# Random-feature attention and two dense layers on one core: keys first, query chunks beside the first layer, and the first layer in two halves of its features

## The chip, the cores and the metric

The kernel runs on one core of a Trainium2 chip. The time is the device time of one execution in microseconds; three executions of the kernel before gave 988.63, 992.81 and 994.16, median 992.81. TensorE is called PE here, VectorE DVE, ScalarE ACT, GpSimd POOL and SyncE SP; all DMAs are issued by SP, in the order of its queue.

## The reference

Inputs are q, k, v (4 batches, 8 heads, 576 tokens, 64 wide), omega (128 by 64) and two pairs of weights. Attention is linear, with random features; then come two dense layers over 2304 tokens with 512 channels and 2048 hidden features, the first with h cos(h), the second with h relu6(h + 3) / 6.

```python
def phi(x):
    proj = np.einsum('bhsd,md->bhsm', x, omega)
    h = proj - np.sum(x * x, axis=-1, keepdims=True) / 2.0
    h = h - np.max(h, axis=-1, keepdims=True)
    return np.exp(h) / np.sqrt(m)
q_p, k_p = (phi(q_s), phi(k_s))
kv = np.einsum('bhsm,bhsd->bhmd', k_p, v)
z = np.sum(k_p, axis=2)
num = np.einsum('bhsm,bhmd->bhsd', q_p, kv)
den = np.einsum('bhsm,bhm->bhs', q_p, z)[..., None] + 1e-06
...
h = x @ w_in
g = h * np.cos(h)
...
g = h * np.clip(h + 3.0, 0.0, 6.0) / 6.0
return (g @ w_out).astype(np.float32)
```

The weights come as 64-bit floats and are turned into 32-bit ones bit by bit on the chip.

## The kernel before

**Precision.** The layers and the projection of the attention are made with operands split into a high part, rounded to the fp32r format, and a low part, the rest. One product is three matmuls: high with high, low weight with high, high with low.

**Attention.** The 2304 tokens are 18 chunks of 128. `att_unit` (L298) makes one unit: keys or queries of one chunk, four of the eight heads. It loads the chunk transposed (xT) and as it lies (nat), squares nat on ACT or POOL and sums it on DVE (sq), splits xT on POOL (th, tl), projects with six matmuls of 256 columns (L359, on an omega that stands twice, block by block on the diagonal), takes maxima (L369) and two bias steps (L373, L377) on DVE, and the exponentials on ACT (L388). A key unit ends in the sums kv over its tokens (L400), a query unit in transposes (L427), a copy (L430), numerators (L440), division (L450 to L461), and after both halves transposes (L475) into xx (L480), the input of the first layer. Queries run six chunks behind the keys, unit by unit interleaved.

**Layers.** A slot is one block of tokens with one chunk of 128 hidden features: 12 matmuls into h (L614), the function, 12 matmuls out of it (L697) that accumulate in four PSUM banks y over all 16 feature chunks of the block. Blocks of the first layer are 512, 512, 256, 512 and 512 tokens, of the second 512 four times and 256. The cosine costs nine steps (L630 to L684): two on ACT and one on DVE or ACT to find the number of turns, two on DVE to take it off, absolute value, sine and rounding on ACT, product and low part on DVE (low part on POOL in the first 16 slots). A weight half (512 columns) is a load of 512 KB, a magnitude (on ACT in the first layer), four steps on DVE (L532 to L548), the rounding wh on ACT and the low part wl on POOL (L569). The halves of 11 of the 16 feature chunks have their buffers where the attention's buffers were, so they are written after the last xx.

**Order.** Nothing is left to chance: `Plan` (L68) is a list scheduler that writes one order for all engines. Each task has a key, durations by engine, what it waits for, and ring buffers that it takes and frees; at each moment the free engine takes the ready task with the smallest key. BIAS shifts the keys of some kinds of tasks. On the chip each engine then runs its own list strictly in that order, waiting on semaphores.

## Time and profile before

| | us |
|---|---|
| median of three runs | 992.81 |
| the profiled execution, its span | 988.6 |
| PE, DVE, ACT, POOL busy | 946.7, 649.2, 497.1, 239.3 |
| first matmul of the first layer starts at | 145.2 |
| block 0 of the first layer, to the start of block 1 | 116.6 |
| each full block of the second layer from 672.1 on | 87.0 |

The span of the profiled execution is close to the fastest of the three runs. The slices show the span in 40 parts of 24.7 us. A window cut at the first matmul of each block shows how long the block took; PE's busy time says little, since the ends of pipelined matmuls are modelled, so matmuls are best read by the distance of their starts. The same holds for DVE and ACT, whose neighbouring instructions overlap in the timeline.

### The profile page before, as it was taken

The numbers are of one execution on the slowest core, as the hardware profiler recorded it, in microseconds if no ns is written. First come the engines' busy times: TensorE is split into PE (matmuls) and PEld (weight loads), VectorE is DVE, ScalarE is ACT, GpSimd is POOL, SyncE is SP. The second block draws the span as 40 slices with busy tenths as digits, with TensorE's granted clock in tenths as the row PEclk, the third lists the DMA queues.
The fourth block names the chain that finished last, engine by engine and source line by source line (L and its number), as shares of the span: only waits on it lengthen the run. The fifth ranks groups of instructions, "written<-read, shape, count | busy, mean of one in ns | idle before, by whom it ended". The sixth has DMA issues, their size and how long they took to land.

```text
span 988.6 us, 15131 instructions
## 1 busy us (share of the span) xinstructions
PE 946.7 (96%) x5714; PEld 792.7 (80%) x5714; DVE 649.2 (66%) x1267; ACT 497.1 (50%) x1010; POOL 239.3 (24%) x270
## 2 busy tenths in 40 slices
PE   8999799988799999999999999999999999999998
PEld 7888687766588889988887778788888888888898
DVE  7999998999995566755699999823223222322322
ACT  6888789666655455544455553323223322322332
POOL 7778844556510000000134234300000000000000
PEclk9999999999999999999999999999999999999999
DMA  9774422344330000000023324101000100100010
GB/s 342 245 237 150 129 63 88 107 128 130 104 107 0 1 1 2 1 1 1 1 59 94 104 73 141 43 0 43 1 1 1 43 1 0 43 1 1 1 43 23
DMA packets 25480, 63.11 MB, mean 64 GB/s; under 512 B 2752, under 2 KB 3776, under 8 KB 25408
## 3 DMA queue, kind: packets, MB, share of 16 engines
q1 hardware_dynamic: 25408, 62.15, 19.5%
q8 instruction: 45, 0.74, 0.3%
q14 instruction: 27, 0.22, 0.1%
HBM read 57.42 MB, written 4.72 MB: 63 GB/s over the span
## 4 chain that ended last, share of the span: by engine, by line
PE 60%; DVE 32%; issue 5%; ACT 2%; DMA 1%; SPq 0%; POOL 0%; DVEq 0%; ACTq 0%
PE h L614 28%; PE pt L697 14%; PE kv L697 14%; DVE wt L542 4%; DVE r L647 3%; DVE wt L532 3%; DVE mx L369 3%; DVE wt L548 3%; DVE wt L536 3%; DVE r L643 2%; DVE mx L373 2%; PE h L359 1%; DVE sq L334 1%; DVE wk L658 1%; DVE gl L257 1%
## 5 line engine op out<-in xcount | busy, mean ns | idle before, releaser
L614 PE MATMUL h<-mxl,wh 128*128 128x512 f32 (+1 forms) x640 | 237.0, 370 | 3.9 <-DVE mxl L257 3.9
L614 PE MATMUL h<-mxh,wl 128*128 128x512 f32 (+1 forms) x640 | 236.9, 370 | 2.1 <-POOL wl L257 2.0
L614 PE MATMUL h<-mxh,wh 128*128 128x512 f32 (+1 forms) x640 | 238.1, 372 | 0.2 <-ACT wh L250 0.2
L257 DVE TENSOR_TENSOR gl<-wk,gh 128x512 fp32r<-128x512 f32 (+1 forms) x144 | 93.8, 651 | 100.3 <-ACT gh L250 93.3
L250 ACT ACTIVATE gh<-wk 128x512 fp32r<-128x512 f32 (+1 forms) x160 | 93.8, 586 | 126.4 <-PE pt L697 101.9
L614 PEld LDWEIGHTS h<-mxl,wh 128*128 128x128 f32 x640 | 121.2, 189 | 26.1 <-DVE mxl L257 6.0
L675 DVE SCALAR_TENSOR_TENSOR wk<-wk,h 128x512 f32<-128x512 f32 (+1 forms) x80 | 50.8, 635 | 138.1 <-ACT wk L669 138.0
L614 PEld LDWEIGHTS h<-mxh,wl 128*128 128x128 f32 x640 | 121.5, 190 | 23.1 <-POOL wl L257 3.2
L614 PEld LDWEIGHTS h<-mxh,wh 128*128 128x128 f32 x640 | 121.5, 190 | 20.8 <-ACT wh L250 0.7
L252 POOL TENSOR_SCALAR mxh<-xx 128x512 fp32r<-128x512 f32 (+1 forms) x20 | 15.9, 799 | 494.2 <-PE h L614 273.3
L257 POOL TENSOR_TENSOR wl<-wt,wh 128x512 fp32r<-128x512 f32 x64 | 97.6, 1528 | 151.7 <-ACT wh L250 140.2
L697 PE MATMUL kv<-gl,wh 128*128 128x512 f32 (+1 forms) x320 | 119.5, 374 | 7.3 <-POOL gl L257 3.8
L697 PE MATMUL kv<-gh,wh 128*128 128x512 f32 (+1 forms) x320 | 118.9, 372 | 4.1 <-ACT gh L250 3.3
L697 PE MATMUL kv<-gh,wl 128*128 128x512 f32 (+1 forms) x320 | 118.7, 371 | 3.5 <-POOL wl L257 3.3
L669 ACT ACTIVATE wk<-h,three 128x512 f32<-128x512 f32 (+1 forms) x80 | 51.5, 644 | 138.7 <-PE h L614 138.7
L697 PE MATMUL pt<-gl,wh 128*128 128x512 f32 (+1 forms) x320 | 119.2, 373 | 0.0
L697 PE MATMUL pt<-gh,wl 128*128 128x512 f32 (+1 forms) x320 | 119.1, 372 | 0.0
L697 PE MATMUL pt<-gh,wh 128*128 128x512 f32 (+1 forms) x320 | 119.0, 372 | 0.0
L651 ACT ACTIVATE r<-r 128x512 f32<-128x512 f32 (+1 forms) x80 | 47.1, 589 | 112.8 <-DVE r L647 112.8
L388 ACT ACTIVATE P<-h,mx 128x128 f32<-128x128 f32 x288 | 81.4, 390 | 19.0 <-DVE mx L377 16.6
L658 DVE TENSOR_TENSOR wk<-h,r 128x512 f32<-128x512 f32 (+1 forms) x80 | 50.7, 634 | 46.2 <-ACT r L655 45.8
L697 PEld LDWEIGHTS kv<-gl,wh 128*128 128x128 f32 x320 | 60.3, 188 | 21.5 <-DVE gl L257 6.5
(70 smaller groups left out, 1583.2 us busy)
## 6 DMA issues: line engine op xcount, KB each, us to landing
ws<-w SPq DMA_DIRECT2D x64, 512.0 KB, 3.7
v<-vn SPq DMA_DIRECT2D x18, 260.0 KB, 4.7
nat<-kn SPq DMA_DIRECT2D x18, 256.0 KB, 4.0
nat<-qn SPq DMA_DIRECT2D x18, 256.0 KB, 3.7
xT<-qT SPq DMA_DIRECT2D x18, 256.0 KB, 3.2
xT<-kT SPq DMA_DIRECT2D x17, 256.0 KB, 4.7
yT<-xx SPq DMA_DIRECT2D x9, 256.0 KB, 2.6
yT<-xx SPq DMA_DIRECT2D x4, 512.0 KB, 2.7
```

What stands on the lines that cost most here:

```text
L250: nc.scalar.activation(out=o, in_=i, func=ACTF.Copy)
L257: (nc.gpsimd if e == "p" else nc.vector).tensor_tensor(out=o, in0=a, in1=b, op=ALU.subtract)
L369: nc.vector.tensor_reduce(out=mx[:, 0:4], in_=pj, axis=AX.X, op=ALU.max)
L388: nc.scalar.activation(out=p[:, o], in_=pj[:, o], func=ACTF.Exp, scale=SCALE, bias=mx[:, 8 + h:9 + h])
L532: nc.vector.tensor_scalar(out=w, in0=w, scalar1=F64_TINY, scalar2=F64_HUGE, op0=ALU.max, op1=ALU.min)
L542: nc.vector.scalar_tensor_tensor(out=u, in0=buf[("ws",) + W][:, :, 1], scalar=SIGN_HI, in1=u, op0=ALU.bitwise_and, op1=ALU.bitwise_or)
L614: nc.tensor.matmul(out=hb(), lhsT=w[:, 128 * kc:128 * kc + 128], rhs=x, start=(kc == 0 and j == 0), stop=(kc == KC - 1 and j == 2),)
L651: nc.scalar.activation(out=r, in_=r, func=ACTF.Abs)
L658: nc.vector.tensor_tensor(out=buf[WK][:, :n], in0=hb(), in1=buf[R_][:, :n], op=ALU.mult)
L669: nc.scalar.activation(out=tile_of(sb, WK, "wk", [128, 512])[:, :n], in_=hb(), func=ACTF.Relu, bias=three)
L675: nc.vector.scalar_tensor_tensor(out=w, in0=w, scalar=6.0, in1=hb(), op0=ALU.min, op1=ALU.mult)
L697: nc.tensor.matmul(out=buf["y", bi, ec][:, :n], lhsT=w[:, o], rhs=x, start=(f == 0 and j == 0), stop=(f == NF - 1 and j == 2),)
```

## The change

- **Stages.** All 18 key chunks run first, then the 18 query chunks, a whole chunk (8 heads) at a time. Beside the query chunks runs part of the first layer: the first 1024 tokens in four blocks of 256, for feature chunks 0 to 7, two feature chunks per "pair slot" in one PSUM bank (48 matmuls of 256 columns). A period is two query chunks; the sines of two pair slots follow the exponentials of their period and come before those of the next (`period`, `prior`, `sn_after`), so ACT changes its table twice a period.
- **Two halves.** The first layer is made for features 0 to 7 over all tokens (mode "pair" for the first 1024, "part" for 512, 512 and 256 more), and its half sums, scaled, go through yp to yy in DRAM; then features 8 to 15 (mode "add") load them back and add. Only the weights of features 8 to 15 (16 halves instead of 22) wait for the attention's buffers.
- **Attention.** No nat loads and no split: the squared sums come from PE (matmuls of the squared xT with a mask), the projection is eight plain fp32 matmuls of 128 columns on 64 rows each, the even heads from partitions 0 to 63 into one bank, the odd ones from 64 to 127 into another. Bias steps are once per chunk, 8 wide.
- **Cosine.** The attention's output is divided by 2 pi, h is in turns, and the cosine is two steps on DVE, a sine on ACT, product, rounding and low part; the factor comes back at the evacuation of y.
- **Weights.** The magnitude is always made on ACT, and wl may go to POOL or DVE; in the emitted order all of it is on DVE. POOL has 275 instructions before and 65 now.
- **Constants.** Rings and banks are divided anew, BIAS is empty, the table of units is gone.

```diff
+N_LATE = 8
+NG = NF - N_LATE
...
+T_K = 3.1
+T_Q = 17.0
...
+    "at": 2, "pt": 2, "h": 2, "kv0": 1, "kv1": 1, "ws": 3, "wt": 3, "mxh": 4, "mxl": 4, "wk": 3, "gh": 2, "gl": 2, "yp": 3,
 }
-Y_BANKS = ["kv0", "kv1"] + ["pt"] * (6 - N_H)
...
+Y_BANKS = ["kv0", "kv1", "h", "h"]
+BIAS = {}
...
+        def sums(e):
+            p = bank(S0, sr)
+            for i in range(4):
+                nc.tensor.matmul(
+                    out=p[:, i:8:4], lhsT=buf[SX][:, 128 * i:128 * i + 128], rhs=mask, start=True, stop=True,
+                )
...
+            for i in range(4):
+                for o in range(2):
                     nc.tensor.matmul(
-                        out=p[:, 256 * i:256 * i + 256], lhsT=w[:, 128 * i:128 * i + 128], rhs=x,
-                        start=(j == 0), stop=(j == 2),
+                        out=buf["pj", kind, c, o][:, 128 * i:128 * i + 128],
+                        lhsT=buf[X][64 * o:64 * o + 64, 128 * i:128 * i + 128],
+                        rhs=omd[64 * o:64 * o + 64, :], start=True, stop=True,
                     )
...
+    for c in range(NCH):
+        p = c // 2
+        prior = [("sn", g) for g in range(n_a) if period(g) == c // PER - 1]
+        chunk("q", c, t_q + T_Q * p + 3 * (c % 2), prior, 10)
...
+    blocks = [dict(m=1, t0=256 * b, n=256, fs=range(0, NG), mode="pair") for b in range(N_A)]
+    blocks += [dict(m=1, t0=t0, n=n, fs=range(0, NG), mode="part") for t0, n in ((1024, 512), (1536, 512), (2048, 256))]
+    n_g1 = len(blocks)
+    blocks += [dict(m=1, t0=t0, n=n, fs=range(NG, NF), mode="add") for t0, n in ((0, 512), (512, 512), (1024, 512), (1536, 512), (2048, 256))]
...
+        add(("wl",) + W, k, {"p": 1.5, "v": 0.68},
...
+            def r1(e):
+                w = buf[WK][:, :n]
...
+                nc.vector.scalar_tensor_tensor(out=w, in0=w, scalar=MAGIC, in1=hb(), op0=ALU.subtract, op1=ALU.subtract)
...
+        sn_after = [("e", "q", c, hf) for c in range(NCH) for hf in range(2) if c // PER == period(g)]
+        nonlinear(g, 1, k, 512, [("in", g, KC - 1)], sn_after + ([("sn", g - 1)] if g else []))
...
+                    nc.vector.scalar_tensor_tensor(
+                        out=xx[:, ec, t0:t0 + n], in0=buf["y", bi, ec][:, :n], scalar=TWOPI, in1=buf["yp", bi, ec][:, :n],
+                        op0=ALU.mult, op1=ALU.add,
+                    )
```

What the change does to the order is seen best on PE and ACT. PE before, where the first layer begins: the last projections of the attention (L359), transposes of finished queries (L475), the first slot (L614) and transposes of exponentials (L427).

```order
L359 MATMUL h<-omh,th 128x256
L359 MATMUL h<-oml,th 128x256
L359 MATMUL h<-omh,tl 128x256
L475 MATMUL pt<-ident,xn 128x128 x4
L614 MATMUL h<-mxh,wh_74 128x512
L614 MATMUL h<-mxh,wl_75 128x512
L614 MATMUL h<-mxl,wh_74 128x512
L427 MATMUL pt<-ident,P 128x128 x4
```

PE now, in the middle of the query stage, between two slots: L709 is a pair slot's matmul into h (wh_83 of slot 13, wh_85 of slot 14), L479 the transposes of query chunk 14, L325 the squared sums and L348 the projection of chunk 16, L431 the transposes and L444 the numerators of chunk 15.

```order
L709 MATMUL h<-mxl,wh_83 128x256
L479 MATMUL pt<-ident,xn 128x128 x4
L325 MATMUL pt<-mask,sqx 128x2 x4
L348 MATMUL at<-omd,xT 128x128 x8
L431 MATMUL pt<-ident,P 128x128 x8
L444 MATMUL pt<-kvs,qt 64x65 x16
L709 MATMUL h<-mxh,wh_85 128x256
L709 MATMUL h<-mxh,wl_86 128x256
L709 MATMUL h<-mxl,wh_85 128x256
```

After these come the other 15 of the 18 matmuls into h, 24 out of slot 12, transposes, 24 out of slot 13 and six more into h of slot 14. The attention's steps moved between the slots of the layer, where before all projections were over when the layer began.

ACT before, around the only change of its table after the start: the turns of the first slots (L637), roundings of weights (L250), copies (L480, L430), an absolute value (L651), the sine (L655).

```order
L637 ACTIVATE wk<-wk,nmagic 128x512
L250 ACTIVATE wh_74<-wt 128x512
L250 ACTIVATE wh_82<-wt 128x512
L480 ACTIVATE xx<-pt 128x4x128
L430 ACTIVATE qt<-pt 128x512
L651 ACTIVATE r<-r 128x512
L430 ACTIVATE qt<-pt 128x512
L655 ACT_TABLE_LOAD
L655 ACTIVATE r<-r,halfpi 128x512
```

ACT now, one period: exponentials (L386) of query chunks 14 and 15, squares (L318), copies of transposes and of finished queries (L249 qt, xx), the sines (L659) and roundings (L249 gh) of slots 12 and 13.

```order
L386 ACT_TABLE_LOAD
L386 ACTIVATE P<-at,mx 128x128 x8
L318 ACTIVATE sqx<-xT 128x512
L249 ACTIVATE qt<-pt 128x512 x2
L386 ACTIVATE P<-at,mx 128x128 x8
L249 ACTIVATE xx<-pt 128x4x128
L659 ACT_TABLE_LOAD
L659 ACTIVATE wk<-wk,halfpi 128x512
L249 ACTIVATE qt<-pt 128x512
L659 ACTIVATE wk<-wk,halfpi 128x512
L249 ACTIVATE gh<-wk 128x512 x2
```

The sines stand between the exponentials of two periods now, where before all exponentials were over. On DVE the two steps of slot 13 (L649, L655) stand ahead of the copy of the squared sums of chunk 16 (L330), its maxima (L361) and a copy of transposes (L253).

```order
L465 TENSOR_TENSOR xn<-pt,rd 128x4x64
L458 RECIPROCAL rd<-rd 128x4
L465 TENSOR_TENSOR xn<-pt,rd 128x4x64
L649 TENSOR_SCALAR wk<-h 128x512
L655 SCALAR_TENSOR_TENSOR wk<-wk,h 128x512
L330 COPY sq<-pt 128x8
L361 TENSOR_REDUCE mx<-at 128x4
L253 COPY qt<-pt 128x512
L662 TENSOR_TENSOR wk<-h,wk 128x512
```

The slot's product (L662) moved behind the maxima of the query chunk; both streams share the one list.

## Rows read from the trace of the kernel before

**Rows 1.** The page: the busy times of the engines, and DVE in 40 slices.

```profile
PE 946.7 (96%) x5714; PEld 792.7 (80%) x5714; DVE 649.2 (66%) x1267; ACT 497.1 (50%) x1010; POOL 239.3 (24%) x270
...
DVE  7999998999995566755699999823223222322322
```

**Rows 2.** Windows cut at the first matmul of a block, of the instructions of L614 alone (the matmuls into h): stretch, its length, PE busy and count, weight loads busy and count, granted clock, share of the DMA engines, GB/s.

```profile
145.20:261.80 116.60, 52.91 (x192) 37.22 (x193) 0.94 0.37 113
261.80:354.90 93.10, 46.83 (x193) 36.05 (x194) 1.00 0.13 40
...
672.10:933.20 261.10, 138.35 (x576) 108.12 (x577) 1.00 0.03 13
```

**Rows 3.** Timeline of the second layer: start and length in us, engine, line, instruction, in brackets the idle time before it. First neighbouring matmuls of 512 columns, then the first two of the last block (256 columns), then the last matmul into an h and the ACT step that waits for it.

```profile
927.83 0.39 PE L614 MATMUL h<-mxh,wh 128*128 128x512 f32 x1
928.05 0.39 PE L614 MATMUL h<-mxh,wl 128*128 128x512 f32 x1
...
933.27 0.28 PE L614 MATMUL h<-mxh,wh 128*128 128x256 f32 x1
933.38 0.28 PE L614 MATMUL h<-mxh,wl 128*128 128x256 f32 x1
...
977.50 0.28 PE L614 MATMUL h<-mxl,wh 128*128 128x256 f32 x1
...
977.88 0.48 ACT L669 ACTIVATE wk<-h,three 128x256 f32<-128x256 f32 x1 [1.20 <-PE h L614]
```

**Rows 4.** Windows of DVE over the attention and the first block: stretch, length, DVE busy and count, granted clock of PE, DMA share, GB/s.

```profile
0.00:145.20 145.20, 136.54 (x394) 0.99 0.59 195
145.20:200.00 54.80, 48.81 (x91) 0.97 0.34 106
200.00:262.00 62.00, 62.00 (x86) 0.92 0.39 119
262.00:300.00 38.00, 34.93 (x60) 1.00 0.32 98
```

**Rows 5.** Timeline of DVE, in the attention and in the change of weights between the layers: start, length, line, instruction.

```profile
86.71 0.68 DVE L369 TENSOR_REDUCE mx<-h 128x4 f32<-128x512 f32 x1
87.31 0.67 DVE L334 TENSOR_REDUCE sq<-nat 128x8 f32<-128x512 f32 x1
87.90 0.15 DVE L373 SCALAR_TENSOR_TENSOR mx<-mx,sq 128x4 f32<-128x4 f32 x1
87.97 0.68 DVE L369 TENSOR_REDUCE mx<-h 128x4 f32<-128x512 f32 x1
...
599.18 0.41 DVE L526 TENSOR_SCALAR wt<-ws 128x512 uint32<-128x512 uint32 x1
599.51 0.68 DVE L542 SCALAR_TENSOR_TENSOR wt<-ws,wt 128x512 uint32<-128x512 uint32 x1
600.12 1.51 DVE L532 TENSOR_SCALAR wt<-wt 128x512 f32<-128x512 f32 x1
```

**Rows 6.** Timeline at 61 us, a POOL instruction and the DVE instruction beside it.

```profile
61.04 1.04 POOL L330 TENSOR_TENSOR nat<-nat 128x512 f32<-128x512 f32 x1
61.19 0.91 DVE L377 SCALAR_TENSOR_TENSOR mx<-mx,sq 128x4 f32<-128x4 f32 x1
```

**Rows 7.** Timeline of ACT: the first exponentials, four exponentials with the two instructions behind them, and the change to the table of the sine.

```profile
10.64 2.18 ACT L388 ACTIVATE P<-h,mx 128x128 f32<-128x128 f32 x8 [0.29 <-DVE mx L377]
...
59.71 1.15 ACT L388 ACTIVATE P<-h,mx 128x128 f32<-128x128 f32 x4 [0.91 <-DVE rd L450]
60.73 0.62 ACT L480 ACTIVATE xx<-pt 128x512 f32<-128x512 f32 x1
61.21 0.66 ACT L328 ACTIVATE nat<-nat 128x512 f32<-128x512 f32 x1
61.73 0.62 ACT L430 ACTIVATE qt<-pt 128x512 f32<-128x512 f32 x1
...
154.31 0.58 ACT L430 ACTIVATE qt<-pt 128x512 f32<-128x512 f32 x1
154.91 1.28 ACT L655 ACT_TABLE_LOAD   x1
156.20 0.72 ACT L655 ACTIVATE r<-r,halfpi 128x512 f32<-128x512 f32 x1
```

**Rows 8.** The page's groups of instructions: the low parts of the weights, all on POOL; busy, mean ns of one, idle time before them and what ended it.

```profile
L257 POOL TENSOR_TENSOR wl<-wt,wh 128x512 fp32r<-128x512 f32 x64 | 97.6, 1528 | 151.7 <-ACT wh L250 140.2
```

**Rows 9.** Timeline of PE in the attention: the last matmul of a projection, key-value sums, numerators, transposes, the next projection.

```profile
57.23 0.28 PE L359 MATMUL h<-omh,tl 128*128 128x256 f32 x1
57.44 0.69 PE L400 MATMUL kv<-v,P 128*64 128x65 f32 x16
57.96 0.64 PE L440 MATMUL pt<-kvs,qt 128*64 128x65 f32 x16
58.52 0.65 PE L475 MATMUL pt<-ident,xn 128*128 128x128 f32 x4
58.94 0.36 PE L359 MATMUL h<-omh,th 128*128 128x256 f32 x1
```

**Rows 10.** Timeline of PE at the start: the ten records of the five plain fp32 matmuls on zeros.

```profile
1.18 4.63 PE L271 MATMUL pt<-zero 128*128 128x256 f32 x10 [1.18 <-DVE zero L268]
```

**Rows 11.** The page's DMA issues: the weight loads, count, KB each, median us from issue to landing.

```profile
ws<-w SPq DMA_DIRECT2D x64, 512.0 KB, 3.7
```

More of the change, by code (lines that the diff above doesn't have):

```diff
@@ L268, in warm @@
         nc.vector.memset(zero, 0.0)
-        p = bank("warm", "pt")
+        p = bank("warm", "h")
         for _ in range(N_WARM):
@@ new lines, in chunk, with period @@
+        add(("xx", c), k + 7.5, {"a": 0.62, "v": 0.65}, put, use=[("xt", c)])
+    for c in range(NCH):
+        chunk("k", c, T_K * c, [], 6)
+    n_a = N_A * NG // 2
+    def period(g):
+        return 1 + g // 2 if PER == 2 else min(3 + g, NCH - 1)
+    for c in range(NCH):
+        p = c // 2
+        prior = [("sn", g) for g in range(n_a) if period(g) == c // PER - 1]
+        chunk("q", c, t_q + T_Q * p + 3 * (c % 2), prior, 10)
+    all_exp = [("e", "q", c, hf) for c in range(NCH) for hf in range(2)]
@@ new lines, in attention_moe_moe2_kernel @@
+    slots = []
+    t = t_m
+    for bi, b in enumerate(blocks):
+        b["g0"] = len(slots)
+        b["t"] = t
+        if b["mode"] == "pair":
+            for fp in range(NG // 2):
+                s = len(slots)
+                slots.append((bi, 2 * fp, t_q + T_Q * (1 + s // 2) + 8 * (s % 2)))
+            b["t"] = slots[b["g0"]][2]
+        else:
+            for f in b["fs"]:
+                slots.append((bi, f, t))
+                t += T_S * b["n"] / 512
+    where = {(bi, f): g for g, (bi, f, _) in enumerate(slots)}
@@ L512, in weight @@
+    n_a = N_A * NG // 2
+    last_w = [None]
+    def weight(src, m, f, hf):
+        W = (m, f, hf)
+        j = 2 * f + hf
+        if m == 1 and f < NG:
+            k = W_K0 + W_KD * j
+        elif m == 1:
+            k = t_m - 8.0 + 5.5 * (j - 2 * NG)
+        elif f < NG:
+            k = blocks[n_g1]["t"] + 10.0 + 9.0 * j
+        else:
+            k = slots[where[n_m1, f]][2] - 30.0
         cols = slice(512 * hf, 512 * hf + 512)
@@ L583, in x_split, with src, view @@
         else:
-            after = [("ev", j, kc) for j, (_, u0, un) in enumerate(blocks[:len(blk1)]) if u0 < t0 + n and t0 < u0 + un]
+            after = [("ev", j, i) for j in range(n_g1, n_m1) if blocks[j]["t0"] < t0 + n and t0 < blocks[j]["t0"] + blocks[j]["n"]]
+        if last_x[0]:
+            after += [last_x[0]]
+        def src():
+            return xx[:, 2 * i:2 * i + 2, t0:t0 + n] if pair else xx[:, i, t0:t0 + n]
+        def view(t):
+            return t.rearrange("p (k t) -> p k t", k=2) if pair else t[:, :n]
@@ L667, in slot @@
+            add(("sn", g), k + 3.3, {"a": a1 + (1.3 if g < n_a and (g == 0 or period(g) != period(g - 1)) else 0.0)}, sn, [("r1", g)] + sn_after, use=[WK])
+            add(("g", g), k + 3.4, {"v": v2}, gg, [("sn", g)], use=[WK, H_])
         else:
@@ new lines, in m_out @@
+                for fi in range(2):
+                    x = slice(256 * fi, 256 * fi + 256)
+                    o = slice(512 + 128 * ec, 512 + 128 * ec + 128)
+                    for j, (w, v) in enumerate(passes(f0 + fi, gh[:, x], gl[:, x])):
+                        nc.tensor.matmul(
+                            out=y, lhsT=w[:, o], rhs=v, start=(first and fi == 0 and j == 0 and ec % 2 == 0),
+                            stop=(last and fi == 1 and j == 2 and ec % 2 == 1), skip_group_check=True,
+                        )
```

645 lines of the change are left out of this document (335 added, 310 removed).

## The prediction

> **What bounds the kernel now.** Three views, in this order: busy times and slices, the layer cut at its block starts, and the timelines of the engines. TensorE (PE) is busy 96% of the span, VectorE (DVE) 66% [rows 1]; that average hides two stages. In the slices DVE stands at 9 from slice 2 to 12 (one 8 among them) and again from 21 to 25; from 27 on it is at 2 or 3 and PE alone is full. Cut at the first matmul of each block, the first-layer matmuls start at 145.2 us [rows 2]. Each of the 128 full slots (512 tokens by one feature chunk) is 24 matmuls, one every 0.227 us: 5.44 us; the 32 slots of 256 tokens take 24 times 0.12, 2.88 us [rows 3]. The floor of both layers is 128 x 5.44 + 32 x 2.88 = 788.5 us. From block 672.1 on the kernel runs at it (261.1 us for three blocks of 87.04). Block 0 takes 116.6 for 87.0, block 1 93.1 [rows 2]. So 988.6 = 145.2 without the layer + 788.5 + 54.9 lost, 29.6 of that in block 0. The change attacks the 145 and the 30.
>
> What is scarce in both is DVE: it is busy 136.5 of the first 145.2 us, 48.8 of the next 54.8, all of the next 62 and 34.9 of 38 [rows 4]. Two things about its price must be read first. Its instructions overlap: one of 128x512 starts 0.60 us after the one before, though it lasts 0.68; a one-source one 0.335 (lasting 0.42); a small one 0.07; a row maximum 0.60 [rows 5]. I count starts. Second, an instruction whose operands are all in SBUF now and then lasts 1.5 instead of 0.42 [rows 5]; in [rows 6] a small one takes 0.91 us, to where GpSimd's (POOL's) ends. POOL's traffic slows DVE. ScalarE (ACT) too overlaps: four exponentials, then the next start 1.02 later, 0.25 each; a rounding 0.52 [rows 7].
>
> **Stage K, the keys.** Per chunk the old DVE work loses the squared sum and its scaling (the sums come from PE), and POOL's two splits go. By the emitted order, up to the last bias of query chunk 0, DVE has 38 maxima and 26 full instructions at 0.60, 18 one-source ones at 0.335, 3 at 0.34 and 59 small ones at 0.075, 50 us; ACT has 152 exponentials at 0.25, 14 roundings and squares at 0.52, 11 magnitudes at 0.56 and 5 copies at 0.27, 54 us with its table load. ACT is the longer. The first exponential now starts at 10.64 [rows 7]; the new chain (load, square, sums, copy, projection, maxima) is as long, so 10.6 again; 50.6 us of ACT lie behind it. DVE idled 6% of 145 to 300 [rows 4]; I take 7% for ACT: 54, **stage K ends at 65**.
>
> **First three query periods.** A period is two query chunks, from period 1 on with two pair slots (256 tokens by two features each: 48 matmuls, 5.76 us). All 16 weight halves of features 0 to 7 fall due by the last of them. DVE up to the low part of slot 3: 10 maxima, 16 sign and low, 8 low parts, 9 copies, 4 input low parts, 16 slot steps, all 63 at 0.60; 29 at 0.335; 39 small: 50.5. The low part of every weight moves from POOL (1.53 us each [rows 8]) to DVE, 0.60 each, and is in these sums; POOL falls from 275 instructions to 65, so I charge 2 us for what is left of its disturbance. 52.5 at 94% is 56: **121**.
>
> **Steady periods.** Here DVE needs 12.3 us per period and ACT 11.3, and the loop through PE is longer. From the end of slot 12's matmuls (X), by the order and [rows 3, 5, 7, 9]: the sums 0.3, transposes 0.44, six matmuls 0.72, projection 1.0 (X+2.4); 0.27 later two maxima and biases to X+4.3; exponentials to X+6.4; PE meanwhile transposes 0.44, two numerators 1.0, 18 matmuls 2.2, transposes 0.44, sums. The next projection waits for the exponentials and for the copy of the sums, which stands behind slot 13's two DVE steps: X+7.7 to 8.7. Eight transposes to 9.6; their copy on DVE to 10.5; numerators to 11.5; 18 matmuls to 13.7; two outputs of 2.88 with transposes between to 19.9; six matmuls to 20.6. With ten changes of matmul shape, at 0.1 (0.21 instead of 0.12 in [rows 9]), part of them inside waits: **20.8 us per period**, 18.5 of it matmul time. The two table loads per period lie beside this loop: sine ends at X+10.5, the low parts at 12.9 and 13.7, and the outputs start at 13.7 and 17.0.
>
> The projection has no row. Bounds: as the transposes, 0.105 per record of 128 columns [rows 9], 16 records: 1.7 us; as the key-value matmuls, 0.52 for 16 records of 65 columns [rows 9], scaled to 128: 1.0; the warm-up's 0.46 per 256 columns [rows 10] gives 3.7, before the clock is on record. I take 1.0: there the two halves of 64 columns alternate, here those of 64 rows. The Trainium skill (TensorEngine Tiling (Array Packing), Key Properties) has tiles of either kind load and multiply independently, which is the 1.0; no run here shows it for rows, and without it the sum is the long loop's below.
>
> A table switch: the sine load of the kernel before starts when the copy ahead of it ends, and the sine 1.29 us later [rows 7]; against the overlap of ordinary instructions 1.4 us in all. The Trainium skill (ScalarE: Activation LUTs, What ACT_TABLE_LOAD costs) speaks against the change here: it adds a drain of 1.38 us to every switch, 2.66 in all; the one switch on record shows none. By the page an estimate of the sum is 10 us more, one drain in each steady period's loop.
>
> **The sum.** Slot 4's matmuls end 6 us after the 121 (two outputs and six matmuls): 127. Five periods to slot 14: 127 + 104 = 231. From there, by the same steps, the last exponentials end 6.4 later, the sines and roundings let the first output of slot 14 start at 12.8, and two outputs of 2.88 with transposes between end at 19. The 512-token blocks start at **250**. What is left is fixed: 16 slots of 5.44 and 8 of 2.88 (110.1), second half of the features 32 and 8 (197.1), second layer 64 and 16 (394.2): 701.4 us. The end stands 9.2 us behind floor time, as now: 933.27 + 46.1 = 979.4 against 988.6 [rows 3]. In the blocks after 250 DVE has 74 us for the 15 slots (82 us of PE) in which the late weights are made, since a cosine slot costs 4 x 0.60 = 2.4 instead of 4 x 0.60 + 0.335; I allow 3 us for losses. 250 + 701.4 + 9.2 + 3 = **964** for an execution like the profiled one, 988.6. The runs' median is 4.2 above that; I add half: **966**.
>
> **At nothing.** The half sums: 20 evacuations and stores and 20 loads of 256 KB or less, while the DMA engines are a fraction busy; landing takes about 3.7 us [rows 11] and an addition is wanted four slots' outputs later than its load can be issued. Four y banks as before. The loads saved (qn, kn) were hidden.
>
> **Rivals.** *Short loop.* The bubbles of the loop close (18.5 plus 1 per period) and K and the first periods run at 98%: 62 + 54 + 6 + 98 + 18 = 238, end 951. Against it: the query banks ("at", two) hold one chunk, so the chain is serial. 0.1.
> *Long loop.* The projection at 1.7 (two per period, 7 loops, and PE becomes longer than ACT in K, 3.5 against 3.0 us a chunk): 10 + 9; or a switch holds ACT for a second 1.29 us [rows 7] in each of 8 periods, because it lets the engine run empty: 10. 975 to 985; the row shows one switch only. 0.2. It is the page's rule on switches, named above, as a mechanism here.
> *Turns instead of overlap, slower than before.* On ACT both sines and both roundings stand between two table loads, and behind them the next chunk's exponentials; if the two streams take turns, a period is two chunk chains of 6.5 (exponentials 2.1, projection 1.0, maxima and biases 2, waits) and one slot chain of 16 (5.76 x 2 and 4.5 of sine, product, rounding, low part): 29, over eight periods 66 us more: 1030. It decides from a period of 24 (3.1 x 8 = 25 us). For it: where the streams met before, 145 to 300, DVE idled 6% though it was the bound [rows 4]; against it the order, which puts PE work of one stream into each wait of the other. 0.08. The same end is reached if PE runs at half clock for 50 us of these stages; it was granted 0.92 where DVE let it wait [rows 4].
>
> **Chances.** Forecast (955 to 974) 0.6, short loop 0.1, long loop 0.2, turns or clock 0.08, not as described 0.02. A measurement tells about 0.5% (5 us of 992.8). Faster by more 0.83, within 0.08, slower 0.09. Range 946 to 990: the short loop's lower end, and the long loop with nearly both its causes (993).
>
> **What would show it.** Right: 512-token blocks from about 250; query exponentials from about 63; periods of 20 to 22 us between sine table loads; DVE instructions near their short durations; second layer at 5.44. Wrong: DVE full through the periods (then its price was read too low), a period of 24 or more, idle PE before the first output of each 512-token block (half sums late), or a granted clock well under 1 in stage K.

## The result and the profile after

The changed kernel takes 1006.92 us (median of 4 runs, 999.12 to 1009.28) against 991.71 for the kernel before (4 runs): a ratio of the means of 1.014, 95% interval 1.0097 to 1.0183. It is slower, by about 15 us, where 966 us were forecast and a range of 946 to 990. The profiled execution has a span of 1005.2 us, the forecast's was 964.

The page of the changed kernel, first the busy times and then three of the lines in 40 slices, answers to [rows 1]:

```profile
PE 979.5 (97%) x6530; PEld 852.3 (85%) x6530; DVE 603.9 (60%) x1202; ACT 430.1 (43%) x866; POOL 47.1 (5%) x60
...
PE   9998899999999999999999999999999999999998
...
DVE  3877778566559998989966589823223222322322
...
PEclk7975789999999999999999999999999999999999
```

DVE and POOL were relieved, as the change meant: 45 us less on DVE, 192 less on POOL. But in slices 0 to 5, the first 150 us, it is now PE that stands at 8 or 9 while DVE stands at 3 to 8, and in the same slices PE's granted clock is 5 to 9 tenths. In the kernel before it was 0.99 over the attention [rows 4].

Windows of the changed kernel, cut where the prediction has its terms: from the first exponential to 63 us, to the first exponential of query chunk 0 (end of stage K), to the end of pair slot 4's matmuls into h, to that of slot 14, to the first 512-token block, to the end. Columns: stretch, length, busy time (and count) of PE, its weight loads, DVE, ACT and POOL, granted clock, DMA share, GB/s.

```profile
10.80:63.00 52.20, 50.90 (x786) 46.59 (x784) 41.95 (x98) 36.43 (x122) 13.68 (x13) 0.89 0.66 210
63.00:90.40 27.40, 26.74 (x284) 24.55 (x284) 17.43 (x41) 15.19 (x49) 4.16 (x4) 0.51 0.38 119
90.40:167.90 77.50, 66.33 (x619) 60.38 (x619) 62.30 (x143) 40.70 (x92) 8.31 (x8) 0.82 0.30 91
167.90:278.90 111.00, 106.30 (x1163) 100.22 (x1162) 66.80 (x173) 62.90 (x141) 4.55 (x6) 1.00 0.12 36
278.90:299.70 20.80, 18.37 (x184) 16.71 (x184) 12.44 (x32) 9.99 (x20) 1.24 (x2) 0.92 0.00 1
299.70:1005.20 705.50, 701.93 (x3458) 596.57 (x3456) 400.79 (x713) 261.05 (x440) 14.57 (x18) 1.00 0.16 50
```

Read the first two rows together: PE is busy 77.6 of 79.6 us, DVE 59.4, ACT 51.6. Stage K is full on PE, and in its second part at half clock (0.51; the two levels are 2.4 and 1.2 GHz). From 300 us on PE is busy 701.9 of 705.5 at clock 1.00: the half sums in DRAM cost nothing there. The whole loss lies before 299.7, where the forecast had 250.

What PE does per key chunk, at full clock and then at half clock (timeline of the changed kernel; start, length, engine, line, instruction; PEld is the weight load):

```profile
41.94 1.16 PE L348 MATMUL at<-omd,xT 64*128 64x128 f32 x16
...
43.03 0.69 PE L401 MATMUL kv<-v,P 128*64 128x65 f32 x16
...
43.65 0.97 PEld L325 LDWEIGHTS pt<-mask,sqx 128*128 128x128 f32 x8
43.65 1.05 PE L325 MATMUL pt<-mask,sqx 128*128 128x2 f32 x8
...
44.63 0.69 PE L401 MATMUL kv<-v,P 128*64 128x65 f32 x16
...
69.06 2.08 PE L348 MATMUL pt<-omd,xT 64*128 64x128 f32 x16
...
71.07 2.20 PE L401 MATMUL kv<-v,P 128*64 128x65 f32 x32
...
73.19 1.87 PE L325 MATMUL h<-mask,sqx 128*128 128x2 f32 x8
74.99 2.00 PE L401 MATMUL kv<-v,P 128*64 128x65 f32 x32
```

The sums, four matmuls of two columns, take 0.98 us from start to start (43.65 to 44.63), nearly as much as the projection of the whole chunk (1.09). A chunk is 1.09 + 0.62 + 0.98 + 0.62 = 3.3 us of PE at full clock, and 2.01 + 2.12 + 1.80 = 5.9 at half.

### The profile page after: what moved, and what is told of

It is laid out like the page before. It is cut to its first block, busy times and chain, and to the rows that moved or that the text cites. A ratio compares the mean times of both kernels' runs of the same rounds, so it can differ in the third digit from the quotient of the medians.

```text
span 1005.2 us, 16174 instructions
## 1 busy us (share of the span) xinstructions
PE 979.5 (97%) x6530; PEld 852.3 (85%) x6530; DVE 603.9 (60%) x1202; ACT 430.1 (43%) x866; POOL 47.1 (5%) x60
## 4 chain that ended last, share of the span: by engine, by line
PE 92%; DVE 5%; issue 2%; ACT 1%; DMA 0%; POOL 0%; SPq 0%; ACTq 0%; POOLq 0%
PE at L778 17%; PE pt L778 17%; PE kv L800 17%; PE h L800 17%; PE h L709 5%; PE kv L735 4%; PE at L348 3%; PE kv L401 2%; PE pt L325 2%; PE pt L444 2%; PE pt L431 1%; DVE mx L361 1%; PE pt L479 1%; PE h L348 1%; PE pt L348 1%
## 5 line engine op out<-in xcount | busy, mean ns | idle before, releaser
L249 ACT ACTIVATE gh<-wk 128x512 fp32r<-128x512 f32 (+1 forms) x160 | 94.1, 588 | 166.3 <-PE h L800 126.8
L778 PE MATMUL at<-mxh,wl 128*128 128x512 f32 (+1 forms) x288 | 105.3, 366 | 0.0
L778 PE MATMUL at<-mxh,wh 128*128 128x512 f32 (+1 forms) x288 | 105.3, 366 | 0.0
L778 PE MATMUL pt<-mxh,wl 128*128 128x512 f32 (+1 forms) x288 | 105.3, 366 | 0.0
L800 PE MATMUL h<-gh,wl 128*128 128x512 f32 (+1 forms) x288 | 105.3, 365 | 0.0
L778 PE MATMUL pt<-mxl,wh 128*128 128x512 f32 (+1 forms) x288 | 105.2, 365 | 0.0
L778 PE MATMUL at<-mxl,wh 128*128 128x512 f32 (+1 forms) x288 | 105.2, 365 | 0.0
L800 PE MATMUL h<-gh,wh 128*128 128x512 f32 (+1 forms) x288 | 105.2, 365 | 0.0
L800 PE MATMUL h<-gl,wh 128*128 128x512 f32 (+1 forms) x288 | 105.2, 365 | 0.0
L778 PE MATMUL pt<-mxh,wh 128*128 128x512 f32 (+1 forms) x288 | 105.2, 365 | 0.0
L659 ACT ACTIVATE wk<-wk,halfpi 128x512 f32<-128x512 f32 (+1 forms) x80 | 54.1, 678 | 88.8 <-DVE wk L655 88.7
L676 DVE SCALAR_TENSOR_TENSOR wk<-wk,at 128x512 f32<-128x512 f32 (+1 forms) x40 | 25.4, 635 | 70.3 <-ACT wk L670 70.2
L800 PEld LDWEIGHTS kv<-gh,wh 128*128 128x128 f32 x288 | 54.4, 189 | 8.8
```

The source lines that it names most:

```text
L249: nc.scalar.activation(out=o, in_=i, func=ACTF.Copy)
L659: nc.scalar.activation(out=r, in_=r, func=ACTF.Sin, scale=-TURN, bias=halfpi)
L676: nc.vector.scalar_tensor_tensor(out=w, in0=w, scalar=6.0, in1=hb(), op0=ALU.min, op1=ALU.mult)
L778: nc.tensor.matmul(out=buf["h", g][:, :n], lhsT=w[:, 128 * kc:128 * kc + 128], rhs=x, start=(kc == 0 and j == 0), stop=(kc == KC - 1 and j ...
L800: nc.tensor.matmul(out=buf["y", bi, ec][:, :n], lhsT=w[:, o], rhs=x, start=(first and j == 0), stop=(last and j == 2),)
```

## The experiments

All times are medians beside runs of the kernel before on the same chip; ratios are of means, and edits are shown shortened. "Fillers" are matmuls of zeros whose result nobody reads. The table takes stage lengths from one trace of each kernel, in us; "first" is the start of query chunk 0's exponentials, the next columns are the lengths from there to the end of slot 4's matmuls into h, to that of slot 14, to the first 512-token block, and to the end.

| | first | to slot 4 | to slot 14 | to blocks | rest | span |
|---|---|---|---|---|---|---|
| forecast | 63 | 64 | 104 | 19 | 713.6 | 964 |
| changed kernel | 90.4 | 77.5 | 111.0 | 20.8 | 705.5 | 1005.2 |
| e1_fill | 81.9 | 82.1 | 118.5 | 21.3 | 705.5 | 1009.3 |
| e8_one_gap | 81.0 | 76.3 | 113.7 | 19.3 | 705.4 | 995.7 |
| e4_sq_act | 80.3 | 73.4 | 115.8 | 20.8 | 705.8 | 996.1 |
| e2_sums | 74.2 | 75.2 | 106.5 | 18.6 | 705.5 | 980.0 |
| e6_sums_act | 71.9 | 72.7 | 107.9 | 18.6 | 705.8 | 976.9 |
| e9_less_w | 68.5 | 69.8 | 110.8 | 19.7 | 705.4 | 974.2 |
| e11_w_early | 81.3 | 70.3 | 104.9 | 18.6 | 705.8 | 980.9 |
| e12_wl_pool | 75.7 | 69.8 | 106.4 | 18.6 | 705.8 | 976.4 |
| e10_h_bank | 73.2 | 68.1 | 107.7 | 20.9 | 705.8 | 975.7 |
| e13_light | 72.7 | 65.0 | 107.8 | 20.8 | 705.8 | 972.1 |
| e14_true_dur | 100.7 | 71.9 | 108.3 | 19.3 | 705.4 | 1005.6 |
| e15_best_dur | 70.4 | 71.1 | 104.6 | 20.1 | 705.4 | 971.6 |
| e16_best_light | 69.2 | 71.5 | 104.6 | 20.0 | 705.4 | 970.7 |

**e1_fill, e2_sums, e3_fill_sums: the clock and the sums.**

```diff
 # e1: in proj, ahead of the projection's matmuls
+for _ in range(2):
+    nc.tensor.matmul(out=p[:, 0:512], lhsT=fill[:, 0:128], rhs=fill, start=True, stop=True)
 # e2
-mask = ap.tile([128, 2], F32, name="mask")
+mask = ap.tile([128, 2], bfloat16, name="mask")
-    t = tile_of(ap, SX, "sqx", [128, 512])
+    t = tile_of(ap, SX, "sqx", [128, 512], bfloat16)
 # e3: both
```

> Ahead of every projection two matmuls of 512 columns of zeros (bf16) are put into the bank that the projection then overwrites; nothing else changes. They are work that nobody needs, 0.23 us each if a 512-column matmul costs here what it costs in the layers, so 36 x 0.46 = 17 us more TensorE time. Theory A (the granted clock): in the changed kernel TensorE stood at 0.50 from about 9 to 23 us, 63 to 98, 102 to 118 and 126 to 136, and this is what most of the lost time is made of. Then the fillers hold the clock near 1.0, key chunks take 3.8 us each (3.3 now at full clock plus 0.46), the first exponential of query chunk 0 comes at about 79 instead of 90.4 us, the 512-token blocks start at about 275 instead of 299.7 and the span is about 980, faster than the changed kernel in spite of the added work. Theory B (waits): the clock is only a sign of TensorE waiting for VectorE and ScalarE; then the fillers change the clock and not the time from 90 us on, and the span is 995 to 1005.

> The squares and the mask are stored as bf16, so that the four matmuls of two columns that make the half squared sums of a chunk run in one pass instead of two: 4 records of about 0.1 us instead of 8 that took 1.05 us together at full clock and 1.87 at half. Theory A (TensorE bounds the key stage, by a term that the prediction read as 0.3 us): a key chunk takes 2.6 us instead of 3.3 at full clock and 4.7 instead of 6.2 at half, a steady period loses 1.3 us; query chunk 0's first exponential at about 75 instead of 90.4, 512-token blocks at about 275, span about 980. Theory B (ScalarE or VectorE takes over at once as the key stage's bound, as the prediction had it, and the loop through TensorE hides the sums behind waits): key stage 3.0 us a chunk, first query exponential at 83 or later, periods unchanged at 22, span 993 to 1000.

> Both edits at once: two 512-column matmuls of zeros ahead of every projection, and squares and mask in bf16. If the lost time is the granted clock and the sums, the gains add up: key chunks 3.0 us each, first query exponential at about 66, 512-token blocks at 250 to 260, span 955 to 970, which would be the time that the prediction had. If waits between the engines bound the first three query periods, blocks start at 275 or later and the span is 980 or more.

e1 takes 1010.33 us, ratio 1.0201 (1.0176 to 1.0227); e2 981.57, 0.9912 (0.9883 to 0.994); e3 987.67, 0.998 (0.9963 to 0.9996). The fillers did hold the clock (1.00 from 11 to 82 us in e1) and query chunk 0 came 8.5 us earlier, as theory A had it to 3 us. But the later stretches grew by 4.6, 7.5 and 0.5 us, together more than that, and in the first query periods the fillers did not hold the clock (0.79, against 0.82 without them). Theory A's total (980) was wrong, and e3's as well (955 to 970). e2 came out as theory A had it: 74.2 for the 75 expected, span 980.0. Timeline of PE in e2, with the weight loads of one set of sums:

```profile
31.83 1.16 PE L348 MATMUL h<-omd,xT 64*128 64x128 f32 x16
32.92 0.69 PE L401 MATMUL kv<-v,P 128*64 128x65 f32 x16
33.54 0.17 PEld L325 LDWEIGHTS <-sqx 128*128 128x128 bf16 x4
33.54 0.25 PE L325 MATMUL at<-mask,sqx 128*128 128x2 bf16 x4
33.73 0.69 PE L401 MATMUL kv<-v,P 128*64 128x65 f32 x16
34.49 1.16 PE L348 MATMUL at<-omd,xT 64*128 64x128 f32 x16
```

The sums take 0.19 us from start to start, not 0.98; the chunk 2.66, not 3.3. bf16 halves the records (eight to four), but that is not the whole of it: by starts a record takes 0.12 us in fp32 and 0.05 in bf16. The eight weight loads last 0.97 us of the matmuls' 1.05, the four 0.17 of 0.25, which points to the load as the price, though the runs do not separate it from the multiply of two columns. The Trainium skill (TensorE: Matmul & The Clock Gate, Weight-path perf modes — Fast Weight Load (FWL) and DoubleRow) states that weights of 128 columns are loaded faster when they are not fp32; the rows agree, with four loads in 0.17 us for eight in 0.97.

**e4_sq_act: the query chunks' squares on ACT.**

```diff
-add(SX, k - 1.5, {"a": 0.6, "p": 1.1}, square, ...)
+add(SX, k - 1.5, {"a": 0.6, "p": 1.1} if isk else {"a": 0.6}, square, ...)
```

> The squares of the query chunks are made by ScalarE alone (0.63 us each) instead of by GpSimd, which made most of them in 1.04 to 1.57 us each while VectorE instructions beside it lasted 1.26 instead of 0.42. Theory B (VectorE's order and GpSimd's disturbance set the pace of the first query periods, 90 to 160 us): some 12 us of VectorE time come back, half of them on the path, blocks start about 6 us earlier, span 999. Theory A (clock and TensorE): at most 2 us, span 1003 to 1006; below no change, since ScalarE then has 11 us more ahead of its exponentials: up to 1010.

998.34 us, ratio 1.0125 (1.0047 to 1.0202), span 996.1: better than both theories, and for a reason that neither had. (One of its four runs took 1011.91.) Query chunk 0 comes at 80.3, ten microseconds earlier, though no query period had begun; the first periods gain 4.1 and the steady ones lose 4.8. The gain is in stage K. There one wait of PE got shorter, 0.36 us for 0.67, and the clock did not fall. That suggested the next run.

**e8_one_gap: 0.7 us of work nobody needs, in one wait.**

```diff
+if c == 13 and hf == 0 and r0 == 0:
+    for _ in range(5):
+        nc.tensor.matmul(out=p[:, 264:512], lhsT=fill[:, 0:128], rhs=fill[:, :248], start=False, ...)
 # then key chunk 13's key-value matmuls into p[:, 0:260], as before
```

> The changed kernel with five matmuls of 248 columns of zeros (bf16, about 0.6 us in all) added at one place: ahead of the first key-value matmul of key chunk 13, where TensorE stood still for 0.67 us at 62.0 us and its granted clock fell to 0.50 one microsecond later, to stay there until 97. Nothing else differs. Theory A (a single wait costs the clock, and the low clock then keeps TensorE the bound): the clock stays at 1.00 until about 80 us, the first exponential of query chunk 0 comes at about 81 instead of 90.4 us, and the span is 8 to 10 us shorter, 995 to 997, for 0.6 us of work that nobody needs. Theory B (the clock is a sign and not a cause; the stage after 62 us is slow because its weights' work on VectorE is): no change, 1003 to 1006.

999.89 us (6 runs), ratio 1.0105 (1.0081 to 1.0129), span 995.7. Timeline of PE in the changed kernel, in brackets the idle time and what ended it:

```profile
60.84 1.15 PE L401 MATMUL kv<-v,P 128*64 128x65 f32 x32
62.66 1.10 PE L401 MATMUL kv<-v,P 64*64 64x65 f32 x16 [0.67 <-ACT P L386]
63.70 2.08 PE L348 MATMUL at<-omd,xT 64*128 64x128 f32 x16
65.70 1.86 PE L325 MATMUL pt<-mask,sqx 128*128 128x2 f32 x8
...
87.74 2.00 PE L401 MATMUL kv<-v,P 128*64 128x65 f32 x32
90.79 1.25 PE L431 MATMUL pt<-ident,P 128*128 128x128 f32 x4 [1.05 <-ACT P L386]
```

and in e8 (its lines are shifted: L354 is the projection, L331 the sums, L409 key-value):

```profile
61.31 1.15 PE L409 MATMUL kv<-v,P 128*64 128x65 f32 x32
62.39 0.70 PE L286 MATMUL kv<-fill 128*128 128x248 bf16 x5
63.13 1.11 PE L409 MATMUL kv<-v,P 64*64 64x65 f32 x16
64.17 1.16 PE L354 MATMUL at<-omd,xT 64*128 64x128 f32 x16
65.26 1.05 PE L331 MATMUL pt<-mask,sqx 128*128 128x2 f32 x8
```

Projection and sums take 1.16 and 1.05 here, 2.08 and 1.86 there. Windows of both, the changed kernel first:

```profile
63.00:70.00 7.00, 7.00 (x76) 6.44 (x78) 5.12 (x14) 4.45 (x16) 1.04 (x1) 0.55 0.55 162
70.00:80.00 10.00, 10.00 (x117) 9.05 (x113) 5.64 (x12) 6.11 (x21) 1.04 (x1) 0.50 0.35 108
80.00:90.00 10.00, 9.74 (x98) 9.05 (x96) 6.28 (x14) 4.42 (x13) 2.08 (x2) 0.50 0.31 107
```

```profile
63.00:70.00 7.00, 6.96 (x126) 6.14 (x125) 6.78 (x19) 6.20 (x21) 1.04 (x1) 1.00 0.75 192
70.00:80.00 10.00, 8.76 (x165) 7.98 (x164) 9.80 (x23) 9.08 (x30) 2.55 (x3) 1.00 0.68 209
```

Between 63 and 80 PE is busy 17.0 us in the changed kernel and 15.7 in e8, and does 193 records and 291. In these two traces the chain is: one wait of 0.67 us, after it the lower level of 1.2 GHz, at that level PE is the bound, and though it does not pause from 62.66 to 89.7 the clock does not come back. Query chunk 0 comes 9.4 us earlier, the span is 9.5 shorter, theory A's numbers. The two intervals of the ratio overlap, since the changed kernel's own runs spread over 10 us: one took 999.12 without any filler, and three of e8's six took 1002 to 1003. So the clock does not fall alike in every run, and chance is not excluded as the reason why it held in the one trace of e8; the traces carry the reading, not the medians. Nor does a wait of this length always bring the fall. In e2 the clock stood at 1.00 through waits of 0.90 and 0.65 us and fell only at 54.4, at the end of one of 1.77:

```profile
47.01 1.16 PE L348 MATMUL pt<-omd,xT 64*128 64x128 f32 x16 [0.90 <-DVE sq L330]
50.24 1.16 PE L348 MATMUL h<-omd,xT 64*128 64x128 f32 x16 [0.65 <-DVE sq L330]
54.45 0.89 PE L401 MATMUL kv<-v,P 64*64 64x65 f32 x10 [1.77 <-ACT P L386]
```

**e5_fill_q, e6_sums_act, e7_all: the first query periods.** e5 is e2 with fillers where PE waits in the periods of query chunks 0 to 5, e6 is e2 and e4 together, e7 is e6 with e5's fillers.

```diff
 # e5, query chunks 0 to 5 and pair slots 0 to 3
+fills(p, 2, True)      # ahead of the transposes of the exponentials
+fills(p, 4, True)      # ahead of those of the normalized chunk
+fills(buf["h", g][:, 256:512] if q else o, 4, q != 1)   # ahead of a slot's first three pieces
```

> On top of the bf16 squares (span 980.0 in that run, granted clock 0.60 to 0.89 between 70 and 120 us): matmuls of zeros where TensorE waits in the first query periods, none in the key stage: four of 512 columns ahead of the transposes of the normalized chunk and two ahead of those of the exponentials (query chunks 0 to 5), four of 256 columns ahead of the first three pieces of pair slots 0 to 3. About 6 x 1.8 + 12 x 0.5 = 16 us of added work, some 10 of it in waits. Theory A (the clock holds the first periods back): the clock is above 0.9 from 75 to 150, about 30 us at half clock become 15, so 15 us come back and about 6 of the fillers' own time is lost: blocks at 265 instead of 274.5, span 971. Theory B (waits on VectorE and ScalarE hold them back, the clock is a sign): the clock rises and the time does not fall, blocks at 275 to 281, span 980 to 987.

> bf16 squares and mask, and the query chunks' squares by ScalarE alone: the two edits that made the kernel faster, together. If GpSimd's squares cost time by themselves (VectorE instructions of 1.26 instead of 0.42 us beside them), the gain of 9 us adds to that of 25: span 971 to 975. If the 9 us were only the clock that happened not to fall at 63 us, which the cheap sums had already changed, little adds: 978 to 983.

> All together: bf16 squares and mask, query squares by ScalarE, and the fillers in the first query periods. Theory A: clock above 0.9 throughout, blocks at about 258, span 962 to 968. Theory B: no better than without fillers, 975 to 985.

e5 984.93 (0.9947, 0.9929 to 0.9964), e6 978.05 (0.9878, 0.9861 to 0.9896), e7 982.32 (0.9923, 0.9904 to 0.9941). Windows of the first periods (chunk 0's exponentials to slot 4's matmuls) in e2 and in e5:

```profile
74.20:149.40 75.20, 63.51 (x601) 56.95 (x601) 61.82 (x143) 40.72 (x93) 8.72 (x9) 0.82 0.31 94
```

```profile
72.60:152.90 80.30, 71.50 (x687) 59.36 (x696) 61.73 (x144) 40.92 (x93) 8.40 (x9) 0.94 0.29 88
```

The clock rose from 0.82 to 0.94 and the stage grew by 5 us: 17 us of fillers (48 of 512 columns, 48 of 256) cost more than the clock gave, as theory B said of the time. Whether a cheaper way to hold the clock pays was left to e13. e6 lies between its two expectations: 3.1 us of span, not 9.

**e9_less_w, e10_h_bank, e11_w_early, e12_wl_pool: VectorE's throughput or a serial loop.** All on e6.

```diff
 # e9: features 4 to 7, clamp, shift, sign and low part become empty steps
+skip = m == 1 and f < NG and j >= 8
 # e10
-pr = ("at", "pt", "h")[c % 3] if isk else "at"
+pr = ("at", "pt", "h")[c % 3] if isk else "h" if c == 1 else "at"
 # e11
-W_KD = 5.2
+W_KD = 4.0
 # e12
-add(("wl",) + W, k, {"p": 1.5, "v": 0.68}, ...)
+add(("wl",) + W, k, {"p": 1.5} if m == 1 and f < NG else {"p": 1.5, "v": 0.68}, ...)
```

> On top of the bf16 squares and ScalarE's squares (span 976.9, query chunk 0 projected at 66.6 us, query chunk 6 at 133.1): the eight weight halves of features 4 to 7 are left as the magnitudes that ScalarE writes; their clamp, shift, sign and low part on VectorE are left out, so those weights and the output are not the reference's. That takes 8 x (2 x 0.335 + 2 x 0.60) = 15 us of VectorE's work out of the first three query periods and nothing else. Theory C (each of these periods is one serial loop through TensorE, ScalarE and VectorE, and the weights' instructions stand in front of the loop's on VectorE): part of the 15 us lies on the loop, the 66.5 us become 56 to 60, span about 968. Theory D (VectorE's throughput bounds them, as the prediction had it): all 15 us come off, 51 us, span 962. Theory E (the loop alone, weights beside it): 65 to 66.5, span 975 to 977.

> On top of the same kernel: query chunk 1 is projected into the two h banks, which are free until pair slot 0, and not into the at banks in which query chunk 0 still stands, so the second chunk of period 0 need not wait for the exponentials of the first. Theory C or E (serial loop, because the banks hold one chunk): period 0, 18.0 us from chunk 0's projection to chunk 2's, shrinks by 4 to 6 us, span 971 to 973. Theory D (VectorE's throughput): no change beyond 1 us, 976 to 978.

> On top of the same kernel: the due times of the first 16 weight halves are 4.0 instead of 5.2 us apart, so that more of their work stands in the key stage, on VectorE as the order has it one to two halves earlier at the start of the query chunks; the total work is the same. Theory D (VectorE's throughput bounds the key stage and the first periods): no change, 975 to 978. Theory C: the key stage gets longer by 2 to 3 us, the first periods shorter by 4 to 6: 973 to 975. If the key stage is bound by VectorE now and the periods by the loop alone, it is slower: 979 to 981.

> On top of the same kernel: the low parts of the first 16 weight halves are made by GpSimd (1.53 us each in the kernel before) instead of VectorE (0.60 each), the place where the kernel before had them. VectorE loses 16 x 0.60 = 9.6 us of work in key stage and first periods. If VectorE's time is what counts and GpSimd's traffic costs little, span 968 to 972. If GpSimd slows the VectorE instructions beside it as it did in the kernel before (1.5 instead of 0.42 us), the gain is eaten: 975 to 982.

e9 975.94 (0.9847, 0.9807 to 0.9888), e10 975.66 (0.9839, 0.9809 to 0.987), e11 983.42 (0.9927, 0.9901 to 0.9953), e12 978.31 (0.987, 0.9829 to 0.991). From chunk 0's projection to chunk 6's, e6 takes 66.5 us, e9 62.8, e10 62.6. Of the 15 us of DVE work that e9 leaves out, 3.7 come back: theory D, the prediction's, falls, C expected too much, and E (the loop alone) is nearest. (Chunk 0's projection also came 3.3 us earlier in e9, at 63.3, though the first step that is left out stands at 66.9 in e6; stage K has the lower clock for 3 us there, for 7 in e6. So the spans of the two do not measure the work left out.) The separate banks of e10 give 3.9, but only 1.5 of it in period 0, where 4 to 6 were expected, the rest in period 1; PE stands at the lower clock for less of these periods too, 17 us for 24 up to slot 4. e11 lengthens stage K by 9.4 us and shortens the first periods by 2.4; its mean clock in stage K is 0.81 for e6's 0.94, so the 9.4 do not show what the moved work costs. e12 changes nothing in the time that can be measured: its stage K is 3.8 us longer, its first periods 2.9 and its steady ones 1.5 shorter.

**e13_light, e14_true_dur, e15_best_dur, e16_best_light.** e13 is e10 with twelve fillers instead of 96, e14 the changed kernel laid out with the durations that its trace shows, e15 the same for e10, e16 both.

```diff
 # e13, on e10
+if c == 0 and hf == 0: fills(p, 3, True)   # ahead of the first transposes
+if c < 3: fills(p, 3, True)                # ahead of the normalized chunk's
 # e14 (e15 keeps the sums at 0.3)
-sums {"t": 0.3}    proj {"t": 0.9}     kv, num {"t": 0.5}
+sums {"t": 1.05}   proj {"t": 1.16}    kv, num {"t": 0.6}
```

> On top of the kernel with bf16 squares, ScalarE's squares and query chunk 1 in the h banks (span 975.7; granted clock 0.78, 0.71, 0.83, 0.83 in the four tens from 70 to 110 us): three matmuls of 512 columns of zeros ahead of the first transposes of query chunk 0 and ahead of the transposes of the normalized query chunks 0 to 2, where TensorE waits 1.3 to 1.9 us; 12 x 0.23 = 2.8 us of added work, nearly all in waits. Theory A (the low clock lengthens the first query periods): clock above 0.95 from 70 to 110, some 15 us at half clock become 8, span 968 to 971. Theory E (the serial loop through the engines; at either clock TensorE is not what it waits for longest): clock up, span 974 to 977.

> The changed kernel with four planned durations set to what its trace shows at full clock: sums 1.05 instead of 0.3, projection 1.16 instead of 0.9, key-value and numerator matmuls 0.6 instead of 0.5. The work is the same, only the emitted order differs. If the wrong plan caused the waits after which the clock falls, the key stage keeps its clock and the span is 990 to 996. If the work itself is what counts (TensorE is full in the key stage at 3.3 us a chunk in any order), it is 1000 to 1008.

> The best version so far (span 975.7) with projection 1.16 and key-value and numerator matmuls 0.6 in the plan, sums left at 0.3, which the bf16 form keeps (0.24 to 0.35 in its traces). Order matters: 968 to 972; work alone matters: 974 to 978.

> e15_best_dur and the twelve fillers of e13_light together. Theory A: 3 to 7 us below e15_best_dur. Theory E: within 2 us of it.

e13 973.73 (0.9811, 0.9787 to 0.9834), e14 1007.13 (1.0141, 1.011 to 1.0172), e15 972.45 (0.9797, 0.9772 to 0.9822), e16 970.63 (0.9782, 0.9759 to 0.9806). The first periods of e10 and of e13:

```profile
73.20:141.20 68.00, 58.01 (x585) 52.41 (x585) 56.68 (x139) 42.92 (x98) 3.35 (x4) 0.87 0.31 100
```

```profile
72.70:137.60 64.90, 55.93 (x596) 49.05 (x594) 56.59 (x139) 42.51 (x98) 3.34 (x4) 0.97 0.34 104
```

With 2.8 us of fillers inside the waits the clock goes from 0.87 to 0.97 and the stage from 68 to 65: 3 us are the clock's, half of what theory A asked, by one trace of each; the intervals of e10 and e13 overlap. e14 shows that laying the kernel out with true durations does not help: it is as slow, its stage K 9 us longer and at a mean clock of 0.73. e15's span is 4 us below e10's by its order, again with overlapping intervals. e16 is a further microsecond below, theory E's number, but it does not decide between the theories, since its fillers did not hold the clock. The first periods of e15 and of e16:

```profile
70.40:141.60 71.20, 59.84 (x605) 53.85 (x604) 60.11 (x145) 43.94 (x102) 3.56 (x5) 0.83 0.34 108
```

```profile
69.20:140.70 71.50, 61.68 (x601) 53.17 (x598) 59.78 (x144) 43.94 (x102) 3.55 (x5) 0.86 0.34 108
```

e16 is the fastest version, 2.2% below the kernel before; e15 and e16 overlap in their intervals.

## Why the prediction was wrong

Step by step, with the table's first two rows.

*Stage K, "ACT is the longer, stage K ends at 65".* This step failed. The prediction billed ACT and DVE by instruction and let PE lie beside them; of the added sums it had only a 0.3 that stood on no row. They measure 1.05 (0.98 by starts), which makes PE the longest with 3.3 us per chunk against ACT's 3.0; ACT's own bill held (51.6 us for 50.6). 18 chunks behind the first exponential at 10.8 are 70 us, and 38 us at the lower clock, which lose up to 19, make most of the way to 90.4. The long-loop rival had PE as the longer in stage K, by the projection at 1.7; that measured 1.09, so it named the right engine for a wrong term. e2, which makes the sums cheap and nothing else, takes 25.2 us off the span, with what that does to the clock; e6 against e4, which differ by the sums alone and where the clock does not fall at 63 us in either (it is low for 7 us of stage K in e6, 13 in e4), 19.2.

*The granted clock.* It was named last, as a sign of error and inside a rival of 0.08, and it came true: by the windows above PE stood at the lower level for about 11 + 27 + 28 us of 10.8 to 167.9 (twice the shortfall from 1.00). The rival priced its end at 1030; it gave 1005, since 50 us at half clock lose at most 25 us of work, and these 66 at most 33. One of the falls, at 63 us, is worth 9.5 us by the traces of e8. The list of signs named stage K, and there it came; the reason given, DVE letting PE wait [rows 4], does not fit the fall at 63 us, which followed 0.67 us of waiting for ACT's exponentials.

*First query periods, 64.* 77.5 measured. This step failed too. The bound was taken to be DVE's throughput at 94%; DVE is busy 62.3 of 77.5 us, 80%, and taking 15 us from it returns 3.7 (e9). The reading that fits best, though no run isolates it, is the loop that the prediction worked out for the steady periods, three times 20.8 or 62.4 us, with its sums and its clock. With cheap sums, two sets of banks and the clock held, e13 measures 65.0, near the forecast but by other causes. How the 13.5 us divide between sums, clock and banks in the changed kernel itself is not settled; fillers large enough to hold the clock there (e5) cost more than they gave.

*Steady periods, 104.* Near, with a term mis-sized. 111.0 measured, 22.2 a period for 20.8; the sums are two per period at 0.7 too little, which is 7 us over five if all of it lies on the loop. e2 with its cheap sums measures 106.5, so 4.5 are the sums'; the rest is open, and the two table loads that start behind a wait (below) could be 2.6 of it. e15 measures 104.6. The projection at 1.0 measured 1.09 by starts, inside its bounds.

*Table switches, 1.4.* The price was right, the place not always. Timeline of ACT in the changed kernel, first a switch where ACT is still at work, then one where it waits:

```profile
181.87 0.63 ACT L249 ACTIVATE gh<-wk 128x512 fp32r<-128x512 f32 x1
182.51 1.28 ACT L386 ACT_TABLE_LOAD   x1
183.81 1.14 ACT L386 ACTIVATE P<-at,mx 128x128 f32<-128x128 f32 x4
...
206.25 0.63 ACT L249 ACTIVATE gh<-wk 128x512 fp32r<-128x512 f32 x1 [1.86 <-DVE wk L662]
208.10 1.28 ACT L386 ACT_TABLE_LOAD   x1 [1.22 <-DVE mx L372]
209.39 1.91 ACT L386 ACTIVATE P<-at,mx 128x128 f32<-128x128 f32 x7
```

In the first the load starts when the rounding has ended and the exponential when the load has: no second 1.3 us. So it is in 12 of the 15 switches behind 125 us, where the load starts at most 0.02 us after the instruction ahead of it; in 13 of the 15 the next instruction starts 0.01 after the load. The drain that the Trainium skill (ScalarE: Activation LUTs, What ACT_TABLE_LOAD costs) adds to a switch does not show as a cost of its own here. (The prediction's estimate of 10 us by that page of the Trainium skill is about seven drains of 1.38; for five steady periods the estimate would be 6.9.) But in three of the seven switches to the exponential (139.18, 208.10 and 251.85, the last two in the steady periods) the load stands behind the wait for DVE's biases and starts 0.08 us after the last of them, when ACT had been idle for 1.2 to 8 us. There its 1.3 us stand between the biases and the exponentials, which are steps of the loop, where the prediction had every load beside it; in e15 it is five of seven. An order that issues the load ahead of that wait was not tried.

*Drain 19, and the rest 713.6.* 20.8 and 705.5. The rest is 8 us shorter. The tail of 9.2 counted a lead twice: when the last block's first matmul starts, two slots' outputs of 2.72 us are still to come, 5.4 us that the 701.4 already holds; and the 3 us for losses were not needed. So the error before 299.7 was larger than the 41 us of the span.

*At nothing.* Right: the half sums, their stores and loads are hidden, the rest being 705.4 to 705.8 us in every traced run.

What remains in e6 against the forecast is 9 us in stage K (there DVE, billed at 50, is busy 56.5 of 61.5 us), 9 in the first periods and 4 in the steady ones, less 8 of the rest.

## What to carry to other kernels

When an engine is left out of a stage's bill because it was not the bound, bill it again with every instruction that the change gives it, each by a row; a matmul of two columns is not two columns cheap, and a number without a row is the one to bound first. Where a change takes wide matmuls off TensorE and leaves small ones among short waits, give the granted clock a term of its own, and try some needless work in one wait before moving anything else; in e1 and e5, more than the waits hold cost more than it gave. Look at several runs before a difference of one trace is called the clock's. Ask whether a loop worked out for the steady state already sets the pace of the first rounds. And a table load that stands behind a wait in its queue is beside the loop only while the engine is still at work.
